# Pooling attention and mixture of depths: first two batches separate, dense work of batch 0 in front of the attention of batch 2, constants on GpSimd

## The chip, the cores and the metric

The kernel runs on one core of one Trainium2 chip. The metric is the device time of the program in microseconds (us). Before the change it is 269.25 us, the median of three runs (268.28, 269.25 and 275.01). The engines of the core are named as in the profile: PE is TensorE, DVE is VectorE, ACT is ScalarE, POOL is GpSimd and SP is SyncE, which here issues the direct DMAs.

## The reference

Two steps follow on each other. First comes an attention in which keys and values are averaged over 8 neighbouring positions; then, for each batch, the 128 rows of the result with the highest gate score go through a two-layer network, and the others stay as they are.

```python
B, H, S, D = 8, 8, 576, 64                       # attention
k_p = k.reshape(B, H, S // 8, 8, D).mean(axis=3)
v_p = v.reshape(B, H, S // 8, 8, D).mean(axis=3)
scores = np.matmul(q, k_p.transpose(0, 1, 3, 2)) / np.sqrt(D)
attn = softmax(scores)                            # + 1e-9 in the denominator
x = np.matmul(attn, v_p)                          # then (B, S, H*D) = (8, 576, 512)
...
scores = np.einsum('bsd,d->bs', x, w_gate)        # mixture of depths
out = x.copy()
for b in range(B):
    top_idx = np.argpartition(-scores[b], 128)[:128]
    xe = x[b, top_idx]
    ye = np.maximum(xe @ w1, 0.0) @ w2            # w1: 512x1024, w2: 1024x512
    g = 1.0 / (1.0 + np.exp(-scores[b, top_idx]))
    out[b, top_idx] = xe + g[:, None] * ye
```

All inputs and the output are float32.

## The kernel before

One function, `direct_path`, holds the whole fast path; a second path runs only if a flag computed at the end asks for it. The schedule is written out by hand: every engine runs its instructions in the order in which the program issues them, and the program issues them in a main loop (L528) over units `u`.

**Units, tiles, chunks.** The 576 positions of a batch are 9 tiles of 64. A unit `u` is three tiles, so a batch has three units, and unit `u` belongs to batch `u // 3`. A chunk `a` is two tiles, 128 rows. Two batches have 18 tiles, so nine chunks; the middle chunk of each pair of batches holds the last tile of the even batch in its lower 64 rows and the first tile of the odd one in its upper 64.

**Attention.** `load_k`, `load_q` and `load_v` issue the input DMAs on SP. `pool_k` (L213) and `pool_v` (L230) add up the eight neighbours, on POOL for all batches but the first; `pool_v` then multiplies the pooled values with the gate weights on POOL, and `gate_v` (L243) sums these products on DVE, so that the gate score comes out of the same matmul as the attention. `k_trans` (L219) and `q_trans` (L263) transpose on DVE. `scores(u)` (L274) runs 32 matmuls into four PSUM banks, and ACT takes the exponential of each bank. `attend(a)` (L287) multiplies the exponentials with the pooled values into an accumulator `pA`, of which there are two; `norm(a)` (L298) takes the reciprocal on DVE and writes the normalised rows `xs` (or `xh` for the middle chunk) and the gate scores `ss`. `store_x(a)` (L331) sends two chunks of rows to the output.

**Choosing rows.** `score(b)` (L350) sums gate scores on DVE, and then splits them into three bf16 parts with five small POOL instructions that write columns 2 to 4 of `auxb` (L362 to L366). `row_bcast(b)` (L368) spreads the scores over rows with five PE transposes into banks 0 and 1. `count(b)` (L374) compares on DVE, with counts in an accumulator output. `one_hot(b)` (L389) sums counts with 15 small matmuls and builds a one-hot matrix on DVE. `gather(b)` (L401) multiplies it with `auxb` on PE (L405), takes the row index (L407, L409) and fetches the chosen rows from the output in DRAM by an indirect DMA on POOL (L413); that DMA waits for the stores of its batch.

**Dense work.** `x_trans(b)` (L425) transposes the fetched rows on PE, `hidden(b, part)` (L432) is the first layer in three parts, `finish(b, part)` (L444) the second in three parts, with an addition on POOL (L454) for each and an indirect DMA back (L456) after the last. `gate(b)` (L419) computes the sigmoid with one small instruction each on ACT, POOL and DVE.

**The order.** `at(u, slot, job)` (L465) puts a job into a slot of a unit. In the main loop a unit runs slot 0, its first chunk (half of it if the unit has only one), slot 1, `scores(u + 1)`, the second chunk (or half), slot 2, the norm, `q_trans(u + 2)`, and then slots 3 to 7. With `w = 3 * (b + 1)`, the unit after the last of batch `b`, the jobs of batch `b` lie from `w` on: `row_bcast` and `count` in slot 3 of `w`, `one_hot` in slot 3 of `w + 1`, `gather` in slot 5 of `w + 1`, `x_trans` in slot 5 of `w + 2`, and the six dense parts in slots 4 and 6 of `w + 3` to `w + 5`. POOL's pooling for batch `b + 2` lies in slots 2 and 5 of `w` and slot 2 of `w + 1`. So three batches are in work at one time. The constants of the choosing are computed on DVE by `constants()` (L177) in slot 3 of unit 0. Each dense or choosing step names its PSUM bank by hand (`nb`).

Of the kernel before, what the change touches and what calls it, by code (L numbers as in the profile page):

```python
# [48 lines left out]
def direct_path(ctx, tc, q, k, v, moe_w_gate, moe_w1, moe_w2, moe_capacity, out, flag):  # L49
# [20 lines left out]

    nc = tc.nc
# [23 lines left out]
    NCH = B * NT // 2  # L95
# [21 lines left out]

    nc.vector.memset(vraws[0], 0.0)
    nc.gpsimd.memset(vraws[1], 0.0)
# [10 lines left out]
    load_q(0)  # L130
    load_v(0, 0)
# [23 lines left out]
    for t in kts + vps + vraws[2:]:  # L155
        nc.gpsimd.memset(t, 0.0)
# [20 lines left out]
    def constants():  # L177
        nc.vector.tensor_scalar(ident, diff, 0.0, None, op0=OP.is_equal)
        nc.vector.tensor_scalar(before[:, NC - 2, :], diff, 0.0, None, op0=OP.is_lt)
        nc.vector.memset(ones, 1.0)  # L180
        nc.vector.memset(one32, 1.0)

        ge, q16, q4, hi = (const.tile([C, n], FT, name=x) for x, n in (
            ("ge", C // G - 1), ("q16", 1), ("q4", 1), ("hi", 1)))
        nc.vector.tensor_scalar(ge, steps, 0.0, None, op0=OP.is_ge, op1=OP.add, accum_out=q16)
        nc.vector.tensor_scalar(q4, q16, 4.0, None, op0=OP.mult)
        nc.vector.scalar_tensor_tensor(hi, q16, -float(G), part, op0=OP.mult, op1=OP.add)
        nc.vector.tensor_scalar(hi, hi, float(TG), None, op0=OP.mult)
        for i, a in enumerate(auxb):
            nc.vector.tensor_scalar(a[:, 0 : NC - 1, 0], numbers, 0.0, hi, op0=OP.mult, op1=OP.add)  # L190
            nc.vector.tensor_copy(a[:, NC - 1, 0:1], hi)
            nc.vector.tensor_scalar(a[:, i : i + NC - 1, 1], numbers, q4, None, op0=OP.add)  # L192
            h = (NC - 1) * (1 - i)
            nc.vector.tensor_scalar(a[:, h, 1:2], q16, float(32 - 4 * i), None, op0=OP.add)
# [10 lines left out]
    def bank(i, shape):  # L205

        return psum.tile(shape, FT, name=f"bank{i}", bufs=1)
# [22 lines left out]
    def pool_v(b, g, eng):  # L230
        x = VR[b, g]
        VP[b] = vps[b % 2]
        h = slice(HG * g, HG * g + HG)
        if eng is nc.vector:
            eng.tensor_reduce(out=VP[b][:, h, 0:D], in_=x.rearrange("p h t d -> p h d t"), axis=AX.X, op=OP.add)
        else:
            eng.tensor_tensor(out=x[:, :, 0:4, :], in0=x[:, :, 0:4, :], in1=x[:, :, 4:8, :], op=OP.add)  # L237
            eng.tensor_tensor(out=x[:, :, 0:2, :], in0=x[:, :, 0:2, :], in1=x[:, :, 2:4, :], op=OP.add)  # L238
            eng.tensor_tensor(out=VP[b][:, h, 0:D], in0=x[:, :, 0, :], in1=x[:, :, 1, :], op=OP.add)

        nc.gpsimd.tensor_tensor(out=x[:, :, 2, :], in0=VP[b][:, h, 0:D], in1=wg[:, h, :], op=OP.mult)
# [5 lines left out]


# [25 lines left out]
    def scores(u):  # L274
        b = u // NTH
        p = [bank(i, [128, 2, TS * TL]) for i in range(4)]
# [10 lines left out]
    def attend(a, heads=range(H)):  # L287
        if heads[0] == 0:
            PA[a] = psum.tile([C, 2, 512], FT, name="pA")
        for h in heads:  # L290
            g, n = divmod(h, HG)
            for t in range(2):
                u, i = divmod(2 * a + t, TS)
                nc.tensor.matmul(PA[a][TL * t : TL * t + TL, g, E * n : E * n + E],  # L294
                                 ET[u][h // 2][:, h % 2, TL * i : TL * i + TL], VP[u // NTH][:, h, :],
                                 start=True, stop=True)

    def norm(a):  # L298
        o = PA.pop(a)[:, :, 0 : HG * E].rearrange("p g (n d) -> p g n d", d=E)
        rz = rzall[:, a, :].rearrange("p (g n) -> p g n", g=2)  # L300
        if a % NT == 0:
            SS[a // NT] = work.tile([C, NT, H], FT, name="ss")
        nc.vector.reciprocal(rz, o[:, :, :, D])  # L303
        k = a % NT
        if k == NC - 1:
            XS[a] = work.tile([C, 1, DM], FT, name="xh")
        elif k - (k >= NC) in (0, 2, 4, 6):
            XS[a] = work.tile([C, 2, DM], FT, name="xs")
        else:
            XS[a] = XS[a - 1]  # L310
        nc.vector.tensor_tensor(out=XS[a][:, 0 if XS.get(a - 1) is not XS[a] else 1, :].rearrange("p (g n d) -> p g n d", g=2, d=D), in0=o[:, :, :, 0:D],  # L311
                                in1=rzall[:, a, :].rearrange("p (g n one) -> p g n one", g=2, one=1).to_broadcast(
                                    [C, 2, HG, D]), op=OP.mult)
        nc.vector.tensor_tensor(out=SS[a // NT][:, a % NT, :].rearrange("p (g n) -> p g n", g=2),
                                in0=o[:, :, :, D + 1], in1=rz, op=OP.mult)
# [15 lines left out]
    def store_x(a):  # L331
# [5 lines left out]
        b = 2 * (a // NT)  # L337
        k = a % NT
        if k == NC - 1:
            x = XS[a][:, 0, :]  # L340
            for n in range(2):
                put(b + n, out[b + n].rearrange("(g t) d -> t g d", g=G)[32:TG], x[TL * n : TL * n + TL])
        elif XS.get(a - 1) is XS[a]:
            b += k >= NC
            i = (k - 1) % NC if k < NC else k - NC - 1
            x = XS[a].rearrange("p i d -> p (i d)")
            y = out[b].rearrange("(g t) d -> g t d", g=G)[:, 0:32].rearrange("g (t i) d -> t g i d", i=4)
            put(b, y[:, :, i : i + 2, :].rearrange("t g i d -> t g (i d)"), x)
# [568 lines left out]
```

## Time and profile before

| what | value |
|---|---|
| median of three runs | 269.25 us |
| the profiled execution: its time, its span | 272.41 us, 270.6 us |
| PE busy, share of the span | 223.3 us, 83% |
| PE weight loads busy | 207.3 us, 77% |
| POOL busy | 155.1 us, 57% |
| DVE busy | 137.6 us, 51% |
| ACT busy | 66.5 us, 25% |
| DMA | 46.94 MB, 173 GB/s over the span |

The page's map of the span in 40 slices (6.8 us each) shows where each engine works; a digit is the busy share in tenths, and PEclk is the granted TensorE clock in tenths:

```profile
PE   0396176680699999999999999999999999999970
PEclk9999669656589999999999999999999999999995
DMA  7999997876702636686736276831222203301101
```

From left to right: PE is thinly used in the first ten slices and full in nearly all others. The DMA engines are full in the first seven slices. The granted clock falls to five or six tenths around slices 5 to 6 and 8 to 11.

### The profile page before, as it was taken

What the parts mean: (1) busy time and instruction counts of PE and PEld (TensorE: products, weight loads), DVE (VectorE), ACT (ScalarE), POOL (GpSimd) and SP (SyncE); (2) the same over time, 40 slices, a digit from 0 to 9 for tenths busy, and PEclk for the clock granted to TensorE, in tenths of its full rate; (3) what the DMA queues carried; (4) which work ended last, traced back from release to release, by engine and by line L of the source; (5) the groups of instructions that cost most, each with busy time, mean ns of one, the idle gap of its engine ahead of it and who ended that gap; (6) DMA issues with size and microseconds to landing.
All of it is one profiled execution on the core that took longest, in us unless ns stands there. A gap on an engine that the chain in (4) does not pass through costs nothing.

```text
span 270.6 us, 7289 instructions
## 1 busy us (share of the span) xinstructions
PE 223.3 (83%) x3050; PEld 207.3 (77%) x3050; DVE 137.6 (51%) x387; ACT 66.5 (25%) x162; POOL 155.1 (57%) x193
## 2 busy tenths in 40 slices
PE   0396176680699999999999999999999999999970
PEld 0376165580599799889997998899889999999970
DVE  7859936664064537654755476538554733411000
ACT  2042022211033133323332333223322331212210
POOL 9889706967970229973995299639953103313021
PEclk9999669656589999999999999999999999999995
DMA  7999997876702636686736276831222203301101
GB/s 278 344 354 398 398 354 284 323 274 204 277 13 50 236 88 206 226 263 208 271 65 249 79 217 224 267 95 44 48 71 79 80 18 116 104 2 39 41 0 51
DMA packets 13048, 46.94 MB, mean 173 GB/s; under 512 B 1104, under 2 KB 1104, under 8 KB 10960
## 3 DMA queue, kind: packets, MB, share of 16 engines
q1 hardware_dynamic: 11728, 42.21, 46.1%
q0 software_dynamic: 1280, 4.20, 4.7%
q8 instruction: 26, 0.43, 0.7%
q14 instruction: 14, 0.11, 0.1%
HBM read 34.87 MB, written 11.53 MB: 171 GB/s over the span
## 4 chain that ended last, share of the span: by engine, by line
PE 69%; DVE 13%; DMA 8%; issue 4%; POOL 3%; ACT 0%; POOLq 0%; DVEq 0%
PE bank L452 21%; PE bank L440 18%; PE bank L281 14%; PE pA L294 13%; DMA out_dram<-xs 5%; DVE qt L271 3%; DMA xr<-out_dram,idx 3%; DVE oh L397 2%; PE bank L371 2%; PE bank L428 2%; DVE xs L311 1%; DVE auxb L192 1%; DVE vp L203 1%; PE bank L405 1%; DVE ge L386 1%
## 5 line engine op out<-in xcount | busy, mean ns | idle before, releaser
L281 PE MATMUL bank<-qt,kt 32*128 32x192 f32 x768 | 46.6, 380 | 18.3 <-DVE qt L271 11.7
L440 PE MATMUL bank<-xg,w 128*128 128x128 f32 x512 | 60.5, 277 | 0.0
L452 PE MATMUL bank<-w,ht 128*128 128x176 f32 (+1 forms) x384 | 60.2, 311 | 0.0
L285 ACT ACTIVATE et<-bank 128x384 f32<-128x384 f32 x96 | 39.4, 495 | 81.9 <-PE bank L281 81.9
L440 PEld LDWEIGHTS bank<-xg,w 128*128 128x128 f32 x512 | 58.4, 192 | 0.5 <-ACT et L285 0.5
L452 PEld LDWEIGHTS bank<-w,ht 128*128 128x128 f32 x384 | 55.8, 190 | 0.6
L294 PEld LDWEIGHTS pA<-vp,et 128*64 128x64 f32 x1152 | 42.4, 152 | 15.7 <-issue 14.9
L281 PEld LDWEIGHTS bank<-qt,kt 32*128 32x128 f32 x768 | 38.6, 216 | 20.6 <-POOL sc L168 11.2
L294 PE MATMUL pA<-vp,et 128*64 128x66 f32 x1152 | 49.0, 241 | 6.1 <-DVE rzall L303 4.7
L303 DVE RECIPROCAL rzall<-pA 128x8 f32<-128x8 f32 x36 | 7.5, 207 | 80.3 <-PE pA L294 80.3
L237 POOL TENSOR_TENSOR vraw<-vraw 128x1024 f32<-128x1024 f32 x15 | 35.3, 2354 | 0.9 <-DVE qt L271 0.9
L454 POOL TENSOR_TENSOR y<-y,xr 128x176 f32<-128x176 f32 (+1 forms) x24 | 13.1, 548 | 39.4 <-ACT y L453 39.0
L271 DVE STREAM_TRANSPOSE qt<-qraw 128x512 f32<-128x512 f32 (+1 forms) x48 | 24.5, 551 | 0.0
L442 ACT ACTIVATE ht<-bank 128x384 f32<-128x384 f32 (+1 forms) x24 | 10.9, 456 | 51.9 <-PE bank L440 51.9
L311 DVE TENSOR_TENSOR xs<-pA,rzall 128x512 f32<-128x512 f32 x32 | 22.1, 691 | 1.4 <-DVE rzall L303 0.2
L453 ACT ACTIVATE y<-bank,g 128x176 f32<-128x176 f32 (+1 forms) x24 | 9.7, 403 | 51.2 <-PE bank L452 51.2
L409 POOL TENSOR_SCALAR idx<-tok 128x1 int32<-128x1 f32 x8 | 1.9, 244 | 31.6 <-DVE g L411 31.4
L238 POOL TENSOR_TENSOR vraw<-vraw 128x512 f32<-128x512 f32 x15 | 19.1, 1272 | 1.2
L386 DVE SCALAR_TENSOR_TENSOR ge<-bank,sc,before 128x128 bf16<-128x128 f32 (+3 forms) x40 | 18.2, 498 | 1.6 <-PE bank L371 1.6
L216 POOL TENSOR_TENSOR kraw<-kraw 128x1152 f32<-128x1152 f32 x7 | 18.4, 2634 | 0.1
L362 POOL CAST auxb<-sc 128x5 bf16<-128x5 f32 x8 | 1.6, 202 | 21.1 <-DVE sc L358 10.7
L428 PE MATMUL bank<-ident,xr 128*128 128x128 f32 x32 | 5.3, 292 | 9.2 <-DMA xr<-out_dram,idx 9.2
(85 smaller groups left out, 186.0 us busy)
## 6 DMA issues: line engine op xcount, KB each, us to landing
kraw<-in_k_dram SPq DMA_DIRECT2D x8, 1152.0 KB
qraw<-in_q_dram SPq DMA_DIRECT2D x8, 1152.0 KB
vraw<-in_v_dram SPq DMA_DIRECT2D x16, 512.0 KB
out_dram<-xs SPq DMA_DIRECT2D x16, 512.0 KB
w<-in_moe_w_dram SPq DMA_DIRECT2D x2, 2048.0 KB
vraw<-in_v_dram SPq DMA_DIRECT2D x16, 64.0 KB
out_dram<-xh SPq DMA_DIRECT2D x8, 128.0 KB
wg<-in_moe_w_gate_dram SPq DMA_DIRECT2D x1, 256.0 KB
```

The source lines that it names most:

```text
L216: eng.tensor_tensor(out=x[:, :, 0:2, :], in0=x[:, :, 0:2, :], in1=x[:, :, 2:4, :], op=OP.add)
L237: eng.tensor_tensor(out=x[:, :, 0:4, :], in0=x[:, :, 0:4, :], in1=x[:, :, 4:8, :], op=OP.add)
L238: eng.tensor_tensor(out=x[:, :, 0:2, :], in0=x[:, :, 0:2, :], in1=x[:, :, 2:4, :], op=OP.add)
L271: nc.vector.transpose(out=QT[u][:, :, n : n + m, :].rearrange("p j t c -> p t j c"), in_=x)
L281: nc.tensor.matmul(p[i][:, s, :], KT[b][r, j, s, :], QT[u][r, j, :, G * s : G * s + G], start=(j == 0), stop=(j == 1))
L285: nc.scalar.activation(ET[u][i], p[i], AF.Exp, scale=exp_scale)
L294: nc.tensor.matmul(PA[a][TL * t : TL * t + TL, g, E * n : E * n + E], ET[u][h // 2][:, h % 2, TL * i : TL * i + TL], VP[u // NTH][:, h, :] ...
L311: nc.vector.tensor_tensor(out=XS[a][:, 0 if XS.get(a - 1) is not XS[a] else 1, :].rearrange("p (g n d) -> p g n d", g=2, d=D), in0=o[:, :, ...
L386: nc.vector.scalar_tensor_tensor(x, y, s, m, op0=OP.is_ge, op1=OP.mult, accum_out=CN[b][:, c : c + 1])
L440: nc.tensor.matmul(p[:, n, :], w1[:, d, 128 * f : 128 * f + 128], XG[b][:, d, :], start=(d == 0), stop=(d == DB - 1))
L452: nc.tensor.matmul(p, HT[b][:, f, :], w2[:, f, c], start=(f == 0), stop=(f == FB - 1))
L454: nc.gpsimd.tensor_tensor(out=Y[b][:, c], in0=Y[b][:, c], in1=XR[b][:, c], op=OP.add)
```

## The change

Five things are changed.

- **The first two batches are split.** The middle chunk of the first pair becomes two chunks of 64 rows, so that batch 0 is complete without a tile of batch 1 (37 chunks instead of 36). Batch 0 is scored one unit earlier.
- **The jobs of batches 0, 1 and 2 get slots of their own.** All dense work of batch 0 is put into unit 5, before the attention of batch 2. The dense work of batches 1 and 2 is spread over units 6 to 10 and 11 to 14. Later batches keep their slots. The loop runs slots up to 12. `w2` is loaded in unit 2 instead of unit 1.
- **The score parts become a job of their own, `parts(b)`,** in the slot of `one_hot(b)`, for all batches. `gate(b)` comes after `x_trans(b)` in the same slot.
- **Constants move from DVE to POOL,** ahead of the first loop; three zero fills move from POOL to ACT; the pooling of v for batch 0 is done on DVE in additions. `scores(1)` moves into the loop.
- **`row_bcast` uses a `pA` accumulator** instead of banks 0 and 1; the other steps take the four banks in turn. The counts go into a zeroed tile `cn` and are summed by one reduction.

```diff
-    NCH = B * NT // 2
+    NCH = B * NT // 2 + 1
...
+    for t in vraws[1:]:
+        nc.scalar.memzero(t.rearrange("p h t d -> p (h t d)"))
...
-    for t in kts + vps + vraws[2:]:
+    for t in kts + vps:
         nc.gpsimd.memset(t, 0.0)
...
-    def constants():
-        nc.vector.tensor_scalar(ident, diff, 0.0, None, op0=OP.is_equal)
...
+    nc.gpsimd.memset(rzall[:, NC - 1 : NC + 1, :], 1.0)
+    cn = [const.tile([C, NC, 2], FT, name=f"cn{i}") for i in range(2)]
+    for t in cn:
+        nc.gpsimd.memset(t, 0.0)
+    nc.gpsimd.tensor_scalar(ident, diff, 0.0, None, op0=OP.is_equal)
+    nc.gpsimd.tensor_scalar(before[:, NC - 2, :], diff, 0.0, None, op0=OP.is_lt)
...
+    nc.gpsimd.tensor_scalar(steps, steps, 0.0, None, op0=OP.is_ge)
+    nc.gpsimd.tensor_copy(q16, steps[:, 0:1])
+    for i in range(1, C // G - 1):
+        nc.gpsimd.tensor_tensor(out=q16, in0=q16, in1=steps[:, i : i + 1], op=OP.add)
...
+    turn = [0]
+
+    def bank(shape, i=None):
+
+        if i is None:
+            i = turn[0]
+        turn[0] = (i + 1) % 4
         return psum.tile(shape, FT, name=f"bank{i}", bufs=1)
...
+    CH = []
+    for i in range(B * NT // 2):
+        if i == NT // 2:
+            CH += [(2 * i, None), (None, 2 * i + 1)]
+        else:
+            CH.append((2 * i, 2 * i + 1))
...
+    def parts(b):
 
         a = auxb[b % 2]
+        s = scs[b % 2]
         r1 = work.tile([C, NC], FT, name="r1")
         nc.gpsimd.tensor_copy(a[:, :, 2], s)
...
     def row_bcast(b):
-        SR[b] = [bank(0, [C, NC - 1, C]), bank(1, [C, 1, C])]
+        p = psum.tile([C, 2, 512], FT, name="pA")
+        SR[b] = [p[:, 0, :].rearrange("p (c i) -> p c i", i=C), p[:, 1, 0:C].rearrange("p (c i) -> p c i", i=C)]
...
-        nc.vector.tensor_tensor(out=CN[b][:, NC - 1 : NC], in0=CN[b][:, NC - 1 : NC], in1=CN[b][:, NC : NC + 1], op=OP.add)
+        nc.vector.tensor_reduce(out=CN[b], in_=k, axis=AX.X, op=OP.add)
...
-            at(u + 1, 2, store_x, a)
+            at(*((u + 1, 2) if u != 5 else (u, 5)), store_x, a)
...
-        at(*((w - 1, 3) if b % 2 else (w, 1)), score, b)
-        at(w, 1 if last else 3, row_bcast, b)
-        at(w, 1 if last else 3, count, b)
-        at(*((w, 7) if last else (w + 1, 3)), one_hot, b, 0)
-        at(w + 1, 5, gather, b, 3)
-        at(w + 2, 5, gate, b)
-        at(w + 2, 5, x_trans, b, 2)
-        at(w + 3, 4, hidden, b, 0, 2)
...
+        at(*((w - 1, 3) if b % 2 or b == 0 else (w, 1)), score, b)
+        steps_of = {
+            0: dict(row_bcast=(3, 1), one_hot=(4, 1), gather=(4, 3), x_trans=(5, 3),
+                    dense=((5, 4), (5, 6), (5, 7), (5, 9), (5, 11), (5, 12))),
+            1: dict(row_bcast=(5, 5), one_hot=(5, 8), gather=(5, 10), x_trans=(6, 5),
+                    dense=((6, 6), (7, 4), (8, 4), (9, 4), (9, 6), (10, 4))),
+            2: dict(row_bcast=(9, 3), one_hot=(10, 3), gather=(10, 5), x_trans=(11, 3),
+                    dense=((11, 4), (11, 6), (12, 4), (13, 4), (13, 6), (14, 4))),
+            B - 1: dict(row_bcast=(w, 1), one_hot=(w, 7), gather=(w + 1, 5), x_trans=(w + 2, 5)),
+        }.get(b, dict(row_bcast=(w, 3), one_hot=(w + 1, 3), gather=(w + 1, 5), x_trans=(w + 2, 5)))
+        dense = steps_of.get("dense", [(w + 3 + i // 2, 4 + 2 * (i % 2)) for i in range(6)])
+        at(*steps_of["row_bcast"], row_bcast, b)
+        at(*steps_of["row_bcast"], count, b)
+        at(*steps_of["one_hot"], parts, b)
+        for f in (one_hot, gather, x_trans):
+            at(*steps_of[f.__name__], f, b)
+        at(*steps_of["x_trans"], gate, b)
+        for i, x in enumerate(dense):
+            at(*x, (hidden, finish)[i // 3], b, i % 3)
...
-    at(1, 0, lambda: nc.sync.dma_start(out=w2, in_=moe_w2.rearrange("(a p) n -> p a n", p=128)))
+    at(2, 3, lambda: nc.sync.dma_start(out=w2, in_=moe_w2.rearrange("(a p) n -> p a n", p=128)))
     eights()
-    pool_v(0, 0, nc.gpsimd)
...
+    pool_v(0, 0, nc.vector)
+    pool_v(0, 1, nc.vector)
     q_trans(1)
-    scores(1)
-    pool_v(0, 1, nc.vector)
...
-    at(0, 3, constants)
...
-        if 0 < u < NU - 1:
+        if u < NU - 1:
             scores(u + 1)
...
-        for slot in range(3, 8):
+        for slot in range(3, 13):
             run(u, slot)
```

`attend`, `norm`, `store_x` and `score` are rewritten for the list `CH` of chunks; what they compute per tile stays.

## The prediction

> **What bounds the kernel now.** I read the page first, then busy time by stretch, the list of waits, the chain that ended last, and the timelines of 0 to 90 and 90 to 135 us. Columns of the first view: stretch and its length, busy time per engine, granted TensorE clock, DMA share, GB/s.
>
> ```profile
> core 0: us, PE busy (x) PEld busy (x) DVE busy (x) ACT busy (x) POOL busy (x), PEclk, DMA share, GB/s
> 11.00:21.00 10.00, 9.26 (x106) 8.35 (x108) 5.62 (x7) 3.28 (x8) 9.12 (x7) 1.00 1.01 345
> 21.00:30.00 9.00, 4.02 (x92) 3.54 (x88) 8.86 (x24) 1.64 (x4) 8.69 (x7) 0.94 1.02 400
> 30.00:44.00 14.00, 9.75 (x163) 8.65 (x164) 7.72 (x23) 2.88 (x8) 3.14 (x9) 0.67 0.96 349
> 44.00:58.00 14.00, 8.05 (x129) 6.99 (x130) 11.39 (x32) 2.06 (x6) 13.45 (x10) 0.69 0.84 307
> 58.00:70.30 12.30, 3.09 (x61) 2.75 (x57) 3.50 (x12) 1.72 (x5) 8.03 (x12) 0.64 0.71 256
> 97.00:124.00 27.00, 26.44 (x399) 24.66 (x398) 15.82 (x46) 8.16 (x20) 19.26 (x22) 1.00 0.63 201
> ```
>
> Two regimes. From 70.3 us to the tail TensorE (PE) is full: 26.4 of 27.0 us for one batch. Before that it is busy for 34.2 of 70.3 us, much of it at a low clock. Time can only come from the first 70 us; any new PE wait afterwards costs its full length. Three waits, each met once, shape the early part (total, times, longest):
>
> ```profile
> POOL auxb L362 <- DVE sc L355: 10.4, 1, 10.4
> ...
> PE bank L428 <- DMA xr<-out_dram,idx: 9.2, 1, 9.2
> ...
> POOL xr L413 <- issue: 3.5, 1, 3.5
> ```
>
> GpSimd (POOL) stood 10.4 us at 32 us for batch 0's scores, with batch 2's pooling queued behind. So the index of the first gather came only at 58.21; its transfer waited 3.46 us for no visible reason and took 8.24; PE stood until 70.29. Now a later batch, around the matmuls that read the one-hot (L405):
>
> ```profile
> 102.50 0.20 POOL L362 CAST auxb<-sc 128x5 bf16<-128x5 f32 x1
> ...
> 103.73 2.63 POOL L216 TENSOR_TENSOR kraw<-kraw 128x1152 f32<-128x1152 f32 x1
> ...
> 115.55 0.28 PE L405 MATMUL bank<-auxb,oh 128*128 128x5 bf16 x5 [0.56 <-DVE oh L397]
> ...
> 117.66 0.68 POOL L241 TENSOR_TENSOR vraw<-vp,wg 128x256 f32<-128x256 f32 x1
> 118.43 0.25 POOL L409 TENSOR_SCALAR idx<-tok 128x1 int32<-128x1 f32 x1
> ```
>
> The reader is to see the order on POOL: the score parts (L362 to L366) run **before** 14.5 us of pooling, so L405, which reads them as auxb, does not wait for POOL. The pooling itself ends at 118.3, later than L405.
>
> **What the Trainium skill says.** "TensorE: Matmul & The Clock Gate", section on the array's architectural detail: GpSimd serves its queue strictly in order, and so do ScalarE and VectorE; the 10.4 us above agree. The same page, Part 1: after an idle window of about 3.4 us PE runs at half clock, for about as long once busy again; the trace grants 0.50 from 65 to 75 us, after the stand from 62, and 32 score matmuls take 2.9 us against 1.51 warm. "GPSIMD Engine Reference", section 3: an addition of two tensors is about 1.96 times as slow on GpSimd as on VectorE; here 2637 against 1359 ns (L216), 1.94. Its section 2.1 puts a first call after loading code at about 6 us; the first gather's 3.46 us may be of that kind, which no run shows.
>
> **Part by part, the early phase.** Prices are rows of the page unless said.
>
> Memsets: three of 1.8 us leave POOL for ScalarE. ScalarE has no such row; its copies of 512 and 384 columns (586, 495 ns) extrapolate to 1.7 us, so from 0.7 to about 7.5 us with the 1.28 table load. Its first exponential is at 14.14: 0, and at double price still under 14.
>
> Constants: 6.5 us leave VectorE (22.7 to 29.2 us in the chain). 26 small instructions go to POOL, spaced 0.27 as L362 to L366 are: 7 us. POOL starts 5.4 us earlier for want of the memsets, so it ends near 12.5; its next work, the gate product, needs VectorE's pooling at 13.5. Cost 0; at twice the price first attention slips 6 us.
>
> Pooling v of batch 0: VectorE does it in additions. L216 and L217 give 1.04 ns a column plus 0.16 us: 1.22 + 0.69 + 0.42 = 2.3 us a half, from the landings at 11.1 and 13.1, so to 15.8. Then q_trans(1) 0.95 and gate sums 0.82: 17.6 us, against 17.98. scores(1) now stands between the halves of the first attention, so norm(0) is at 22.4 rather than 20.8.
>
> From there I follow each queue in program order with these prices: a norm 1.05 (L303, L311, L314), q_trans 0.95, k_trans 2.1, counting 3.7 on VectorE; scores 1.5 warm or 2.9 cold, full-chunk attention 1.1 on PE; the four exponentials 1.64. norm(0) and q_trans(2) end at 24.4, exponentials of unit 1 at 23.2, attend(1) at 24.3: norm(1) starts at 24.4 (was 29.1). norm(1), norm(2), q_trans(3) and k_trans(1) on VectorE follow on each other, the second after attend(2) at 27.1: k_trans(1) ends 31.3 (33.9). Then norm(3), gate sum, norm(4), q_trans(4), the scores' sums and the other gate sum reach 36.4; the split chunk adds norm(5), 1.05 us; count(0) runs from 37.5 (45.8). Counting now holds one of the two pA accumulators: attend(7) waits for it until 41.2. One-hot ends at 44.3, and scores(5) waits that long for bank 0; index at 49.1 (58.2). POOL doesn't hold it: parts go behind pool_k(2), and with w2 off SP's queue ahead of them k2 and v2 land about 6 us earlier (2 MB at 345 GB/s), so the pooling of batch 2 ends near 47. w2 lands by 46 and is needed near 73; the stores of batch 0 that it delays land near 47, before the gather.
>
> Repeating the gather's 3.46 + 8.24 us gives x_trans(0) at **61.2**, 9.1 us earlier. Ends: a landing of 3.4 us, this row's minimum, and no 3.46 give 53, where attention still holds PE until 55; a gather no earlier than before gives 70. After it come 0.7 for the XG copy, now uncovered, a cold start (1.5), dense(0) 14.6 and batch 1's counting matmuls: stage u=6 starts near 80 and u=9 at 97.1. The old u=9 started at 100.0, with 7.3 us less of dense done. **Lead 10 us.**
>
> **The late phase.** `parts` moves from `score` to the one-hot's slot, past pool_k, pool_v(.,0) and pool_v(.,1) of batch b+2 on POOL. L405 now waits for these. Using the stage prices 2.75 or 3.7 (attention), hidden 2.68, 2.68, 1.9, finish 2.5, 2.6, 2.2, pooling 4.05 + 5.1 + 5.1, parts 1.3:
> - Batch 2: in POOL's order pool_v(4,0) is behind the addition of finish(1,0), so it starts 8 us into u=9 and parts end at 20.1; PE is at the gather at 15.0. Wait 5.1. The index is then behind an addition and a scatter (1.7), and x_trans(2), moved up to slot 3, waits 2.4 more: 7.5.
> - Batch 3: PE has finish(2,0) in front; parts are 0.8 early: 0.
> - Batch 4: 2.5. Batch 5: 2.6. In the timeline above: POOL from 102.5, pooling to 117.0, parts to 118.3, less 115.55, is 2.75. Batches 6 and 7 have no pooling ahead: 0.
>
> Sum 12.6, less the waits for the one-hot that it swallows (0.6 in four batches): **10.2 lost**. The cold restart after 5 us of standing would add up to 1.7; part of it lies under the wait for x_trans(2): take 1. Below nothing isn't possible: nothing speeds L405. If POOL keeps 3 us more slack it is 4; if each wait is 1.5 longer, 17.
>
> At no cost: the count's last sum (L387, 946 ns) becomes a single-input reduction of some 0.15 us; gate after x_trans holds VectorE about 0.8 us longer. VectorE is busy 15.8 of 27 us, and PE's work covers both. The pA lent to counting is free 3.4 us before the second attention of the next stage needs it (108.6 against 112.0). The banks taken in turn are read before scores want them.
>
> Sum: 270.6 - 10 + 10.2 + 1 = 271.8 span. The profiled execution took 272.41, 3.2 above the median of 269.25; carried over, 270.5. Following the queues ignores small waits: **271**.
>
> **Rivals.** (A, 0.48) As above, gain given back: 271, own range 265 to 275. (B, 0.18) POOL arrives in time, or the first gather lands in 3 to 4 us, so the lead survives: 269.25 - 9.5 = 260. For it: batch 3's slot shows that a PE job in front suffices; against: POOL's pooling ended 2.8 us after L405 already, without the parts behind it. (C, 0.34) The parts' wait outweighs the lead. Place: L405 of batches 2, 4, 5. Price 12.6, or 17 with cold restarts. It decides once the waits exceed the lead by 5.4. With the gather at 66 (lead 5.5), the end is 269.25 + 17 - 5.5 - 2.4 = 278. For it: transfers still fill the DMA engines (0.96 to 1.02) when that gather runs. That dense(0) gets ahead of little, since PE still stands for the gather from 54.5 to 61, is inside A.
>
> **Numbers.** 2% is about what a measurement of this kernel tells from no change: 263.9 and 274.6. A is mostly inside, B faster, C slower: 0.18, 0.48, 0.34. Range 261 to 281: A with most of B and C.
>
> **What would show it.** Right: POOL's 10.4 us gone; first gather's index at 47 to 52 us; x_trans(0) at 59 to 63; L405 waiting for POOL auxb L366 in three late batches, 2 to 5 us each, and PE under 25 of 27 us there. Wrong: no late wait of L405 on POOL (then B), or x_trans(0) after 66 (then C).

## The result, and the profile after

The changed kernel takes 279.38 us, the median of four runs (278.65 to 282.01); the kernel before, run beside it, took 272.13 us (268.28 to 276.58). The ratio is **1.043, 95% interval 1.033 to 1.052: slower**. (A ratio compares undisturbed runs of both kernels only, so here and below it is the quotient neither of the medians nor of the spans: the one profiled execution of the kernel before, 272.41 us, is 3 to 4 us longer than its undisturbed runs of 268.28 and 269.25, while the changed kernel's, 279.86, is 0.5 above its median.) The profiled execution took 279.86 us with a span of 278.1 us, against 272.41 and 270.6 before.

The map of the span, in 40 slices of 7.0 us, for the changed kernel:

```profile
PE   0358566639998999478999995999789999999980
...
PEclk9999879777999999959999998899979999999997
DMA  7999999878120739745745587230312204301101
```

The reader is to see two things. PE is full from slice 10, or 63 us (before: from slice 12, or 74 us). But now there are holes after it, at slices 17, 25 and 29 (from 111, 167 and 195 us), and the granted clock dips at the same places or just behind them. Before, nothing of the kind followed the first 80 us.

Busy time by stretch (stretch and length, PE, PE weight loads, DVE, ACT, POOL, then granted clock, DMA share, GB/s), changed kernel:

```profile
core 0: us, PE busy (x) PEld busy (x) DVE busy (x) ACT busy (x) POOL busy (x), PEclk, DMA share, GB/s
21.00:30.00 9.00, 6.41 (x152) 5.33 (x148) 5.52 (x14) 3.28 (x8) 8.69 (x7) 1.00 1.01 410
...
58.00:70.30 12.30, 8.89 (x57) 8.52 (x58) 4.36 (x17) 1.18 (x3) 1.21 (x6) 0.72 0.77 290
97.00:124.00 27.00, 21.65 (x325) 20.19 (x325) 14.54 (x45) 6.51 (x16) 18.91 (x22) 0.88 0.61 201
```

From 21 to 30 us DVE is no longer full (5.52 us busy, before 8.86), and PE does 6.41 us of work instead of 4.02. From 58 to 70.3 us PE does 8.89 us instead of 3.09. From 97 to 124 us it loses: 21.65 us at a clock of 0.88, where it had 26.44 at 1.00. The list of waits (total, times, longest) of the changed kernel names the cause:

```profile
PE bank L435 <- POOL auxb L394: 11.7, 3, 5.4
...
PE bank L458 <- DMA xr<-out_dram,idx: 3.7, 1, 3.7
POOL xr L443 <- POOL idx L439: 3.6, 7, 0.8
```

L435 is the gather matmul (L405 before), L394 the last score part. Its three waits are new. The 10.4 us for which POOL stood for the scores are gone, the wait for the first gathered rows fell from 9.2 to 3.7 us, and the 3.5 us ahead of the first gather's transfer fell to 0.83. (In the ten traces of the experiments this last wait is 0.7 to 1.8 us, so the 3.5 belongs to the one profiled execution before.) The chain that ended last, by engine, says the same in one line:

```profile
PE 56%; POOL 22%; DVE 8%; issue 5%; DMA 5%; ACT 1%; POOLq 0%; DVEq 0%; ACTq 0%
```

POOL has 22% of it; before it had 3%, and PE 69%.

**The early phase, as forecast.** The timeline around the first gather:

```profile
50.84 0.24 POOL L439 TENSOR_SCALAR idx<-tok 128x1 int32<-128x1 f32 x1 [2.71 <-DVE g L441]
51.91 1.23 POOL L443 DMA_INDIRECT xr<-out_dram,idx  x1 [0.83 <-POOL idx L439]
60.74 1.09 PE L458 MATMUL bank<-ident,xr 128*128 128x128 f32 x4 [3.68 <-DMA xr<-out_dram,idx]
```

x_trans(0) starts at 60.74 us, 9.55 earlier than in the profiled execution before (70.29).

**The late phase.** POOL around the gather matmul of batch 2:

```profile
107.05 0.56 POOL L484 TENSOR_TENSOR y<-y,xr 128x176 f32<-128x176 f32 x1 [5.90 <-ACT y L483]
107.56 2.35 POOL L245 TENSOR_TENSOR vraw<-vraw 128x1024 f32<-128x1024 f32 x1
...
117.88 0.68 POOL L249 TENSOR_TENSOR vraw<-vp,wg 128x256 f32<-128x256 f32 x1
118.51 0.20 POOL L390 CAST auxb<-sc 128x5 bf16<-128x5 f32 x1
...
119.58 0.20 POOL L394 CAST auxb<-r 128x5 bf16<-128x5 f32 x1
```

And PE, in batches 2, 4 and 5 (the last bracket is the idle time before, and for whom); below it, the place of batch 4 in the kernel before:

```profile
112.04 2.44 PE L482 MATMUL bank<-w,ht 128*128 128x160 f32 x16
119.84 0.28 PE L435 MATMUL bank<-auxb,oh 128*128 128x5 bf16 x5 [5.35 <-POOL auxb L394]
120.04 2.03 PE L315 MATMUL pA<-vp,et 128*64 128x66 f32 x32
122.00 2.70 PE L301 MATMUL bank<-qt,kt 32*128 32x192 f32 x32
...
171.35 0.27 PE L435 MATMUL bank<-auxb,oh 128*128 128x5 bf16 x5 [3.05 <-POOL auxb L394]
171.48 4.31 PE L482 MATMUL bank<-w,ht 128*128 128x176 f32 x16
...
202.97 0.27 PE L435 MATMUL bank<-auxb,oh 128*128 128x5 bf16 x5 [3.34 <-POOL auxb L394]
203.10 4.18 PE L482 MATMUL bank<-w,ht 128*128 128x176 f32 x16
```

```profile
169.29 0.28 PE L405 MATMUL bank<-auxb,oh 128*128 128x5 bf16 x5 [0.56 <-DVE oh L397]
169.43 2.63 PE L452 MATMUL bank<-w,ht 128*128 128x176 f32 x16
```

In batch 2 POOL first stands 5.90 us for the input of an addition of batch 1, then works through 11 us of pooling and one more addition, and only then writes the parts; PE stands for the last 5.35 us of this. And the price does not end with the wait. What comes right behind it is slow: 2.03 and 2.70 us for pieces that take 1.16 and 1.58 elsewhere, 4.31 and 4.18 for 16 matmuls of the second layer that take 2.63 in the same places before. The granted clock is 0.57 from 172 to 176 us. Such slow work at a lower clock behind a stand is called a slow or cold restart below.

A subtraction sorts all runs below. Before, 200.3 us lie between the start of x_trans(0) and the end (270.6 - 70.29). In the changed kernel it is 217.4 us (278.1 - 60.74). So the change wins **9.55 us** up to there and loses **17.1 us** after it, which makes the 7.5 us of the two spans. In both kernels PE has the same 2513 matmuls left at that point; the changed kernel is busy with them for 4.6 us more (193.7 against 189.2) and idle for 12.5 us more.

The ratio says more than 7.5: some 11.5 us. The difference is the profiled execution before, which was 3 to 4 us too long. Kernels 7 and 10 below have its code behind x_trans(0) and take 200.2 and 201.9 us there, so the excess most likely lies ahead of it. By this estimate the change wins about 6 us, not 9.55, against the shorter runs, and the loss of 17.1 stands.

### The profile page after: what moved, and what is told of

Read it like the earlier page. It is cut to its first block, busy times and chain, and to the rows that moved or that the text cites. A ratio compares the mean times of both kernels' runs of the same rounds, so it can differ in the third digit from the quotient of the medians.

```text
span 278.1 us, 7308 instructions
## 1 busy us (share of the span) xinstructions
PE 225.4 (81%) x3050; PEld 209.9 (75%) x3050; DVE 126.1 (45%) x378; ACT 72.2 (26%) x165; POOL 155.1 (56%) x213
## 4 chain that ended last, share of the span: by engine, by line
PE 56%; POOL 22%; DVE 8%; issue 5%; DMA 5%; ACT 1%; POOLq 0%; DVEq 0%; ACTq 0%
PE bank L482 19%; PE bank L470 16%; PE bank L301 9%; PE pA L315 9%; POOL vraw L245 6%; POOL vraw L246 4%; DMA xr<-out_dram,idx 3%; POOL kraw L227 3%; POOL vraw L249 2%; POOL vp L247 2%; DMA kraw<-in_k_dram 2%; DVE qt L291 2%; POOL ks L228 2%; PE pA L400 1%; PE bank L458 1%
## 5 line engine op out<-in xcount | busy, mean ns | idle before, releaser
L470 PE MATMUL bank<-xg,w 128*128 128x128 f32 x512 | 62.6, 282 | 2.3 <-ACT xg L460 2.3
L482 PE MATMUL bank<-w,ht 128*128 128x176 f32 (+1 forms) x384 | 63.1, 322 | 0.0
L470 PEld LDWEIGHTS bank<-xg,w 128*128 128x128 f32 x512 | 60.2, 197 | 3.4 <-ACT xg L460 3.2
L301 PE MATMUL bank<-qt,kt 32*128 32x192 f32 x768 | 45.2, 379 | 20.5 <-DVE qt L291 11.2
L482 PEld LDWEIGHTS bank<-w,ht 128*128 128x128 f32 x384 | 59.0, 198 | 0.4
L328 DVE RECIPROCAL rzall<-pA 128x8 f32<-128x8 f32 (+1 forms) x37 | 7.6, 205 | 84.8 <-PE pA L315 84.8
L245 POOL TENSOR_TENSOR vraw<-vraw 128x1024 f32<-128x1024 f32 x14 | 33.0, 2357 | 0.0
L416 DVE SCALAR_TENSOR_TENSOR ge<-pA,sc,before 128x128 bf16<-128x128 f32 (+3 forms) x40 | 18.3, 501 | 5.5 <-PE pA L400 5.5
L435 PE MATMUL bank<-auxb,oh 128*128 128x5 bf16 x40 | 2.2, 167 | 11.8 <-POOL auxb L394 11.7
L249 POOL TENSOR_TENSOR vraw<-vp,wg 128x256 f32<-128x256 f32 x16 | 10.9, 683 | 1.2
```

Source lines behind the costliest of these rows:

```text
L301: nc.tensor.matmul(p[i][:, s, :], KT[b][r, j, s, :], QT[u][r, j, :, G * s : G * s + G], start=(j == 0), stop=(j == 1))
L416: nc.vector.scalar_tensor_tensor(x, y, s, m, op0=OP.is_ge, op1=OP.mult, accum_out=k[:, c, 0:1])
L470: nc.tensor.matmul(p[:, n, :], w1[:, d, 128 * f : 128 * f + 128], XG[b][:, d, :], start=(d == 0), stop=(d == DB - 1))
L482: nc.tensor.matmul(p, HT[b][:, f, :], w2[:, f, c], start=(f == 0), stop=(f == FB - 1))
```

## The experiments

My theory after the result: the early part brings a lead, the moved `parts` lose it in the late phase. The rivals: the split chunk, the new slots or the dense work put ahead cost the time; or it is the clock alone. Ten experiments (7 and 10 are one kernel), each with runs of the kernel before on its own chip; the three columns of times are of the one profiled execution of each:

| kernel | x_trans(0), us | from there to the end | span | ratio to before, 95% |
|---|---|---|---|---|
| before | 70.29 | 200.3 | 270.6 | 1 |
| changed | 60.74 | 217.4 | 278.1 | 1.043 (1.033 to 1.052) |
| 1: parts early, rest changed | 62.95 | 216.9 | 279.8 | 1.049 (1.029 to 1.069) |
| 2: before, parts late | 64.14 | 217.1 | 281.2 | 1.057 (1.045 to 1.069) |
| 3: gather of batches 4, 5 behind finish | 60.44 | 210.6 | 271.0 | 1.015 (0.999 to 1.030) |
| 4: pooling and parts of batch 2 earlier | 61.88 | 211.6 | 273.5 | 1.011 (1.000 to 1.023) |
| 5: as 4, with work ahead of x_trans(2) | 61.63 | 205.5 | 267.1 | 0.989 (0.978 to 1.000) |
| 6: added matmuls keep PE busy | 63.05 | 217.1 | 280.1 | 1.033 (1.021 to 1.045) |
| 7: before, early part alone | 62.51 | 200.2 | 262.7 | 0.985 (0.970 to 1.001) |
| 10: the same again | 62.41 | 201.9 | 264.3 | 0.987 (0.981 to 0.993) |
| 8: as 7, rows and counts as changed | 60.88 | 200.9 | 261.8 | 0.975 (0.970 to 0.980) |
| 9: batch 0 ahead, later slots as before | 58.97 | 205.7 | 264.7 | 0.997 (0.994 to 1.000) |

Seven kernels have the changed kernel's code up to x_trans(0) (changed, 1, 3, 4, 5, 6, 9), and it lies between 59.0 and 63.1 us in them: a difference of two microseconds in that column is not to be read by itself.

**1. The parts behind the scores again, the rest as changed**

```diff
+        if b >= 2:
+            at(*((w - 1, 3) if b % 2 else (w, 1)), parts, b)
...
-        at(*steps_of["one_hot"], parts, b)
+        if b < 2:
+            at(*steps_of["one_hot"], parts, b)
```

> The changed kernel with one thing undone for batches 2 to 7: the five score parts are issued on GpSimd directly behind the sums of score, ahead of the pooling of batch b+2, as in the kernel before. Theory (the parts' place in GpSimd's queue costs the late phase): the waits of L435 for auxb of 3.05 us (batch 4) and 3.3 us (batch 5) go, with the cold restarts behind them (finish(b,0) took 4.2 and 4.0 us instead of 2.5), so about 9.5 us. Batch 2 gains only about 1 us, since its index is still behind pool_v(4,1) and its x_trans is two slots earlier. Span 278.1 - 10 = 268, ratio to before 0.97 to 1.00. Rival (the slots of batches 0 to 2, or the accumulator lent to counting, are the cost): the waits move elsewhere, span 275 or more, ratio 1.02 or more.

282.33 us, ratio 1.049: missed, and the waits moved elsewhere, as the rival had it. All waits of L435 for POOL are gone. But a new one stands in batch 2 (timeline of this kernel):

```profile
116.41 0.28 PE L435 MATMUL bank<-auxb,oh 128*128 128x5 bf16 x5 [0.16 <-DVE oh L427]
...
123.23 1.07 POOL L443 DMA_INDIRECT xr<-out_dram,idx  x1 [0.29 <-POOL idx L439]
123.47 0.34 SPq L111 DMA_DIRECT2D kraw<-in_k_dram  x1
123.92 2.36 SPq L125 DMA_DIRECT2D vraw<-in_v_dram  x1
...
133.98 1.09 PE L458 MATMUL bank<-ident,xr 128*128 128x128 f32 x4 [12.68 <-DMA xr<-out_dram,idx]
```

L435 now runs on time, but the index is still behind POOL's pooling, and x_trans(2) was moved to one unit behind it. The gather leaves at 123.23 us, 0.24 us ahead of the loads of batch 5, and its rows take 10.6 us; the shortest landing in this trace is 3.3. In the changed kernel these loads came only at 127.97, behind a store of attention rows that PE's stand had delayed to 126.80; the gather, issued at 122.23, landed in 3.8 us. One wait was taken away and the one behind it came up, larger. The moved slots of batch 2 are a second fault, hidden behind the first. (That the loads slow the rows is read from these times; no run moves the loads alone.)

**2. The kernel before, with `parts` in the slot of `one_hot` and nothing else**

```diff
+    def parts(b):
+        s = scs[b % 2]
         a = auxb[b % 2]
...
+        at(*((w, 7) if last else (w + 1, 3)), parts, b)
         at(*((w, 7) if last else (w + 1, 3)), one_hot, b, 0)
```

> The kernel before with that one thing done: the score parts are put into the slot of the one-hot, behind the pooling of batch b+2, nothing else. Theory: L405 waits 2.2 to 2.8 us for the parts in each of batches 2 to 5, with about 1.5 us of cold restart behind each and 0.6 us of one-hot wait saved: 4 x 3.4 = 13.6 us slower; the 10.4 us wait of GpSimd at 32 us goes, but gains at most 1 us, since VectorE's chain holds the first gather. Ratio 1.03 to 1.06. Rival (the slots of batches 0 to 2 are the cost): ratio 0.99 to 1.01.

283.39 us, ratio 1.057: as expected. Its PE timeline at batch 4:

```profile
174.51 0.27 PE L408 MATMUL bank<-auxb,oh 128*128 128x5 bf16 x5 [3.37 <-POOL auxb L369]
174.63 4.31 PE L455 MATMUL bank<-w,ht 128*128 128x176 f32 x16
```

Here the sum can be closed. The gather matmul (now L408) stood 3.38, 2.58, 3.37 and 2.56 us in batches 2 to 5, 11.9 in all (the second and fourth are put down to DVE's k_trans, which ended in the same moment as POOL's last part: both at 143.71 in batch 3); less the 0.56 to 0.63 it stood there before, 9.5. The second-layer piece behind it took 5.04, 4.31, 4.31 and 4.04 instead of 2.63: 7.2 more. Together 16.7 us, and the kernel is 16.8 us longer behind x_trans(0) (217.1 against 200.3). Two fifths of the price is the slow restart.

The same edit also took POOL's early stand away, and x_trans(0) came 6.2 us earlier than in the profiled execution before. But the index came only 0.7 us earlier (57.55), as expected. The rest is the transfer: 0.70 us ahead of it instead of 3.46, and 5.50 to land instead of 8.24. So POOL's stand of 10.4 us was not what held the first gather.

**3. The gather of batches 4 and 5 behind the second-layer piece, the rest as changed**

```diff
+        if b in (4, 5):
+            steps_of["gather"] = (w + 1, 7)
```

> The changed kernel with the parts where it has them, but the gather matmul of batches 4 and 5 moved two slots back, behind finish(b-1,0), so that TensorE has 2.5 us of work while the parts are made. Theory (a wait with nothing in front costs its length and a cold restart): the two waits shrink from 3.05 and 3.3 to under 1 us and finish(b-1,0) runs in 2.5 us, so 2 x (2.5 + 1.6) = 8 us: span 270, ratio 0.98 to 1.01. Rival (GpSimd itself is the bound in the late phase, so any order on TensorE ends the same): span 276 or more.

272.36 us, span 271.0, 7.1 us less than the changed kernel: as expected in the span and the mechanism; the ratio of 1.015 lies just above the range. PE at batch 4:

```profile
169.07 2.55 PE L482 MATMUL bank<-w,ht 128*128 128x176 f32 x16
172.31 0.27 PE L435 MATMUL bank<-auxb,oh 128*128 128x5 bf16 x5 [0.69 <-POOL auxb L394]
```

With 2.5 us of other PE work ahead of it, L435 waits 0.69 us for its parts here and 1.02 in batch 5, and the second-layer piece runs in 2.55. The parts are as late as in the changed kernel; only PE's order differs.

**4. Pooling and parts of batch 2 earlier on POOL**

```diff
+        if b >= 3:
+            at(*((w - 1, 3) if b % 2 else (w, 1)), parts, b)
...
-            at(u, 5, pool_v, b + 1, 0, nc.gpsimd)
+            at(u, 3 if u == 9 else 5, pool_v, b + 1, 0, nc.gpsimd)
...
+    at(9, 3, parts, 2)
```

> As the first kernel for batches 3 to 7; and for batch 2, pool_v(4,0) is put in front of the addition of finish(1,0) in GpSimd's queue, with the parts of batch 2 behind it, so that GpSimd doesn't stand 5.9 us at 101 us for that addition. Theory: the wait of L435 in batch 2 (5.35 us) and the cold attention behind it (about 2 us) go too; x_trans(2) may wait 1 to 2 us for its rows. Span 261 to 264, ratio 0.955 to 0.985: faster than before. Rival (the slots of batches 0 to 2 are the cost): 270 or more.

272.24 us, ratio 1.011 (the profiled execution, 275.27, was the longest of its four): missed, about half of the gain that was expected, and the number is the rival's. No wait of L435 is over 0.7 us, but x_trans(2), in its moved slot, waits 4.93 us for rows that took 6.6 to land, and hidden(2) behind it is slow again: its 48 matmuls took about 8.5 us, and 5.5 elsewhere.

**5. The same, with work ahead of x_trans(2)**

```diff
-                    dense=((6, 6), (7, 4), (8, 4), (9, 4), (9, 6), (10, 4))),
+                    dense=((6, 6), (7, 4), (8, 4), (9, 4), (10, 4), (11, 3))),
...
-            at(u + 1, 3, k_trans, b + 1)
+            at(u + 1, 6 if u == 9 else 3, k_trans, b + 1)
```

> The fourth kernel, with x_trans(2) given cover: finish(1,1) and finish(1,2) move to slot 4 of unit 10 and slot 3 of unit 11, the latter in front of x_trans(2), and k_trans(4) moves behind the gather of batch 2, so that its index isn't late. Theory (what was left in the fourth kernel is the 4.9 us wait of x_trans(2) for its rows and the half clock behind it, hidden(2) 8.5 us instead of 5.4): the wait falls under 2 us and hidden(2) runs in 5.4 to 6: 5 to 7 us less than the fourth kernel. Ratio 0.97 to 0.99. Rival (the transfer is only pushed into the loads of batch 5 and ends as late): ratio 1.00 to 1.02.

268.11 us, ratio 0.989: as expected.

```profile
123.69 0.63 PE L458 MATMUL bank<-ident,xr 128*128 128x128 f32 x4 [1.93 <-DMA xr<-out_dram,idx]
124.99 5.62 PE L470 MATMUL bank<-xg,w 128*128 128x128 f32 x48 [0.68 <-ACT xg L460]
```

The wait of x_trans(2) is down to 1.93 us, though its rows took 7.3 to land, and hidden(2) takes 5.62.

**6. Work for PE during the wait.** In batches 4 and 5, 16 matmul calls on the weights, whose result nothing reads, run ahead of the gather matmul of the changed kernel.

```diff
     def gather(b):
+        if b in (4, 5):
+            i = turn[0]
+            p = bank([cap, 176], i)
+            for f in range(FB):
+                for n in range(2):
+                    nc.tensor.matmul(p, w2[:, f, 128 * n : 128 * n + 128], w2[:, f, 0:176],
+                                     start=(f == 0 and n == 0), stop=(f == FB - 1 and n == 1))
+            turn[0] = i
```

> The changed kernel with 16 added matmuls of the shape 128x176 that nothing reads (2.5 us) in front of the gather matmul of batches 4 and 5. TensorE still waits for the same parts, but is busy for most of the wait. Theory (each wait of 3 us has a second price, a cold restart): parts end when they did, so L435 isn't earlier, but finish(b-1,0) behind it runs in 2.5 us instead of 4.2 and 4.0: 3.2 us less in all, ratio 1.02 to 1.035. Rival (no clock effect, the long finish has another cause): finish(b-1,0) stays at 4 us, ratio as the changed kernel's, 1.04.

279.81 us. PE at batch 4:

```profile
169.86 4.94 PE L438 MATMUL bank<-w 128*128 128x176 f32 x32
174.94 0.27 PE L442 MATMUL bank<-auxb,oh 128*128 128x5 bf16 x5
175.07 2.63 PE L489 MATMUL bank<-w,ht 128*128 128x176 f32 x16
```

The added work came out twice as large as meant (the profile counts 32 matmuls), and outlasts the parts, which were written at 173.06, by 1.8 us; so the total tells nothing. The last line does: behind PE that was kept busy the second-layer piece takes 2.63 us, behind PE that stood 3.05 us it took 4.31. (In batch 5 it is 2.63 against 4.18.) From 172 to 176 us the granted clock is 1.00 here and 0.57 in the changed kernel. The restart's price is shown: 1.7 us at this place.

**7. The early part alone.** The kernel before, with the zero fills on ACT, the constants on POOL, the pooling of v for batch 0 by additions on DVE, `scores(1)` in the loop, `w2` in unit 2, all as the change has them, and the late `parts` for batch 0 only. No split chunk, no dense work ahead, slots and banks as before.

```diff
+        if b > 0:
+            parts(b)
...
+        if b == 0:
+            at(w + 1, 3, parts, b)
         at(*((w, 7) if last else (w + 1, 3)), one_hot, b, 0)
```

> The kernel before with the early part of the change alone: constants on GpSimd in the preamble, zero fills on ScalarE, pooling of v of batch 0 on VectorE, scores(1) in the loop, w2 loaded in unit 2, the score parts of batch 0 (only) in the one-hot's slot. Chunks, slots, banks and all other parts stay. Theory (the lead of the changed kernel comes from VectorE and GpSimd being free early, which brings the first gather forward): the first gather's index at 50 to 54 us instead of 58.2, x_trans(0) at 61 to 65 instead of 70.3, span 262 to 266, ratio 0.97 to 0.985. Rival (without the split of the middle chunk and the earlier slots nothing comes forward): x_trans(0) after 68, ratio 0.99 to 1.00.

265.48 us, ratio 0.985: as expected. From x_trans(0) to the end it is the kernel before to 0.1 us (200.2 and 200.3), so the whole gain is the earlier x_trans(0). By the ratio the gain is some 4 us; the 7.8 us between the two profiled executions hold the excess of the one before.

**8. Rows in a pA accumulator and counts in a zeroed tile, on top of 7**

```diff
-        SR[b] = [bank(0, [C, NC - 1, C]), bank(1, [C, 1, C])]
+        p = psum.tile([C, 2, 512], FT, name="pA")
+        SR[b] = [p[:, 0, :].rearrange("p (c i) -> p c i", i=C), p[:, 1, 0:C].rearrange("p (c i) -> p c i", i=C)]
...
-        nc.vector.tensor_tensor(out=CN[b][:, NC - 1 : NC], in0=CN[b][:, NC - 1 : NC], in1=CN[b][:, NC : NC + 1], op=OP.add)
+        nc.vector.tensor_reduce(out=CN[b], in_=k, axis=AX.X, op=OP.add)
```

> The early part alone (median ratio 0.985 in the run before this one, span 262.7) plus two things that the forecast set at no cost: rows for counting in a pA accumulator, and the counts in a zeroed tile summed by one reduction. My theory (no cost, since PE work covers both): span 262 to 264, ratio within 0.01 of the early part alone, which runs beside it. Rival (the pA lent to counting holds the attention back in every batch): 0.5 us or more a batch, span 267 or more, with new waits of the attention matmuls for DVE.

262.60 us, ratio 0.975 (0.970 to 0.980), with 0.987 (0.981 to 0.993) for the early part alone beside it: better than no cost. The intervals do not meet. The scores of unit 5 show where gain comes from; first in the kernel without the two edits (experiment 10), then in this one:

```profile
44.96 3.12 PE L280 MATMUL bank<-qt,kt 32*128 32x192 f32 x32 [3.64 <-DVE ge L387]
```

```profile
43.73 1.58 PE L283 MATMUL bank<-qt,kt 32*128 32x192 f32 x32 [0.16 <-DVE qt L273]
```

In the old order the scores of unit 5 wait 3.64 us for DVE to finish counting in banks 0 and 1, and then run cold. With the rows in pA they run at once. The two edits were not tried apart: the last sum of the counts also fell, from 886 ns in the mean to 166, once a batch on DVE. This is the fastest kernel of this case.

**9. Batch 0 split and its dense work ahead, later slots as before**

```diff
-            1: dict(row_bcast=(5, 5), one_hot=(5, 8), gather=(5, 10), x_trans=(6, 5),
-                    dense=((6, 6), (7, 4), (8, 4), (9, 4), (9, 6), (10, 4))),
-            2: dict(row_bcast=(9, 3), one_hot=(10, 3), gather=(10, 5), x_trans=(11, 3),
-                    dense=((11, 4), (11, 6), (12, 4), (13, 4), (13, 6), (14, 4))),
+            1: dict(row_bcast=(5, 5), one_hot=(5, 8), gather=(5, 10), x_trans=(8, 5)),
```

and `parts` as in 1.

> The changed kernel with the score parts right behind the scores from batch 2 on, and batches 1 and 2 with their dense work (and x_trans) in the slots of all later batches; only batch 0 keeps its own completion and its dense work ahead of the attention of batch 2. Theory that the split and the dense work ahead are worth about as much as the early part alone, and that all of the loss sits in the moved parts and the moved slots of batches 1 and 2: unit 9 begins at 91 to 93 us, span 262 to 266, ratio 0.97 to 0.985. Rival (with dense work of batch 0 out of units 6 to 8, PE there outruns POOL's pooling of batch 3, 14.5 us from about 80): PE waits for keys of batch 3 ahead of unit 9, unit 9 begins at 96 or later, span 267 to 270, ratio 0.99 to 1.0.

268.88 us, ratio 0.997: the span of its one profiled execution, 264.7, is where it was expected, but that was the fastest of 19 runs (266.55 to 272.83), and the ratio missed. So this order is worth nothing that can be seen against before, and is 2.3% slower than kernel 8 on the same chip (0.997 / 0.975). Unit 9 begins at 92.2, as expected; but ahead of it and within it PE waits:

```profile
89.45 1.58 PE L301 MATMUL bank<-qt,kt 32*128 32x192 f32 x32 [3.62 <-DVE kt L239]
...
95.25 0.65 PE L315 MATMUL pA<-vp,et 128*64 128x66 f32 x14 [2.24 <-DVE g L453]
```

The first is for the keys of batch 3: with no dense work between, PE runs ahead of DVE, where the transposition of the keys is queued behind a norm and q_trans. The second is put down to `gate` (L453), but the gate sums of batch 3 run on DVE just ahead of it, from 94.68 us, and had waited for POOL's last product, which ended at 94.65. POOL could begin that batch's pooling only at 80.04, after the last step of the dense work put ahead, and needs 14.6 us for it: the bound that the rival named.

**10. The early part again, with more rounds**

> The early part alone once more, with more rounds, on the chip of the two others: its interval touched 1.0 before. Expected ratio 0.97 to 0.985, span 262 to 264. If the first result was luck of one chip: 0.99 to 1.0.

266.22 us, span 264.3, ratio 0.987 (0.981 to 0.993): just above both expected ranges (ratio and span), but the whole interval lies below 1. A gain of 0.7 to 1.9% is shown on a second chip.

Together: the parts' place alone costs the kernel before 16.8 us behind x_trans(0) (2), by waits that PE can cover (3) and restarts that need PE to stand (6). The rivals are right in part. The moved slots of batch 2 are a second fault (1, 4, 5), and the split chunk with the dense work ahead brings nothing over kernel 8 (9).

## Why the prediction was wrong

The forecast was "gain given back" at 271 us, and 279.38 were measured; what happened is its rival C, the parts' wait outweighing the lead, at its upper price. The place and the cause of the waits were right; terms of the sum were mis-sized, the slow restart most of all.

- **Zero fills on ScalarE, cost 0:** right. They ran from 2.02 to 7.5 us, as worked out.
- **Constants on GpSimd, ending near 12.5:** they ended at 16.14, and the next gate product began at 16.22. Some of the small instructions took 0.7 to 1.3 us instead of 0.2 to 0.3 (last section). It cost nothing visible: norm(0) was forecast at 22.4 and came at 22.41.
- **The early queues:** norm(1) at 24.4 (24.28), k_trans(1) done by 31.3 (31.1), index at 49.1 (50.84), x_trans(0) at 61.2 (60.74). The chain was 1.7 us late by the index; the 3.46 us that I repeated ahead of the transfer were only 0.83, its landing 8.69 instead of 8.24. The two roughly cancelled. That POOL's stand of 10.4 us held the first index was a wrong reading: without it the index came 0.7 us earlier (experiment 2); with DVE freed as well it came at 53.33 (experiment 7). Experiments 7 and 8 show which parts made the lead: by the ratios the early part some 4 us, the rows in pA with the new counts some 3 more. With the split chunk as well x_trans(0) came at 59.0 to 63.1, around the 60.88 of experiment 8, so the split itself bought nothing that can be seen.
- **"Lead 10 us" at u=9:** u=6 began at 79.8, as forecast ("near 80"), but u=9 at 99.66, not 97.1: units 6 to 8 took 19.9 us, not the 17.1 from 80 to 97.1. x_trans(1) waited for the exponentials (0.50), its first reader for the copy (0.98), the scores of unit 9 for the keys (0.62). The lead was 0.34 + 7.3 = 7.6 us.
- **L405 waits for batches 2, 4, 5 and not 3:** right in place, in all four. Batch 2: 5.1 forecast, 5.35 measured. Batches 4 and 5: 2.5 and 2.6, measured 3.05 and 3.34.
- **The failing step: "The cold restart after 5 us of standing ... take 1".** I counted one restart, behind the longest wait, and let x_trans(2) swallow part of it. The runs show three: about 2.0 us behind batch 2 (0.87 + 1.12), 1.68 behind batch 4, 1.55 behind batch 5. That is 5.2 us instead of 1. Experiment 6 shows it by itself, and experiment 2 closes its sum only with it. From u=9 on, 15.1 us were lost where 10.2 + 1 were forecast: the restarts cost 4.2 more and the waits of L435 1.5 more, while the 2.4 for x_trans(2) did not come. With the lead 2.4 short, that is 6.3 us, and 271.8 + 6.3 is the measured span of 278.1.
- **The excess of 3.2 us carried over:** the span was forecast 6.3 us too short, but the time 8.4. The profiled execution before was 3.2 us above the median, and I took this off the changed kernel too, whose profiled execution was only 0.5 above. If the excess lies ahead of x_trans(0), as estimated above, it was in the lead already and was taken off twice.
- **x_trans(2) waits 2.4 more:** in the changed kernel it hardly waits; PE's own stand delays the loads that come beside its rows in experiment 1. That was luck: with the stand gone, it waits 12.7 us there.
- **"At no cost":** the counts' reduction takes 166 ns (946 before), right. The rows in pA, tried together with it, were not neutral but a gain, which I missed: they free the banks that the next scores wait for. The banks in turn and the gate behind x_trans cost nothing visible; neither was tried alone.
- **Rival C's price** was 17 us with cold restarts: 17.1 measured from x_trans(0) on. I gave it an example with a lead of only 5.5 because of a late gather. The gather was not late, and the lead of 9.55 by the profiled executions was not enough either; against the shorter runs it was about 6 by the estimate above, and the end close to the 278 of that example.

On the restart, the Trainium skill ("TensorE: Matmul & The Clock Gate", Part 1) says that PE falls to half clock after an idle window of about 3.4 us. I read this as a threshold that waits of 2.5 us stay under. The trace disagrees with that reading: stands of 2.56 to 3.38 us (experiment 2) already made the next 16 matmuls 1.4 to 2.4 us longer. Nor is it certain above that length: behind the stand of 3.62 us in experiment 9 the granted clock stayed at 1.00 (89 to 93 us) and the 32 score matmuls took 1.58 us. So the length of a stand alone does not tell whether a restart follows. Here the measurement decides.

What stays open: why kernel 9 scatters over 6 us and the kernel before over 10, while kernel 8, run beside them, scatters over 2.7; where the last 5 us of kernel 5 behind x_trans(0) go (205.5 against 200 to 202); and whether kernel 8 gains from a split chunk with slots made for it. This was not tried, nor were the split and the dense work ahead tried apart.

## What to carry to other kernels

When a small step is moved behind long work on another engine's queue, price its wait where PE stands, and allow for a slow restart behind each such stand, even of 2.6 us: in experiment 2 it was two fifths of the loss, though one stand of 3.6 us in experiment 9 had none. Compare the profiled execution with the other runs of its kernel before taking a lead from it. Put other PE work between the late input and its reader (experiment 3 got 7.1 us back in this way without making the input earlier), and look at what the wait you remove was holding back (experiment 1). And take a bundle of edits apart: two groups of its parts were worth 2.5% (experiment 8), and the rest cost more than that.

## What the runs showed of the hardware

**Small instructions on POOL or DVE can last as long as a long one beside them on the other engine.** POOL's constants and DVE's work of the changed kernel, from its timelines:

```profile
6.07 1.32 POOL L188 TENSOR_SCALAR steps<-steps 128x7 f32<-128x7 f32 x1
...
11.02 1.23 POOL L198 CAST auxb<-hi 128x1 bf16<-128x1 f32 x1
...
13.48 1.21 POOL L197 TENSOR_SCALAR auxb<-numbers,hi 128x4 bf16<-128x4 f32 x1
```

```profile
5.92 1.36 DVE L227 TENSOR_TENSOR kraw<-kraw 128x1152 f32<-128x1152 f32 x1 [1.31 <-DMA kraw<-in_k_dram]
...
11.03 1.18 DVE L245 TENSOR_TENSOR vraw<-vraw 128x1024 f32<-128x1024 f32 x1
...
13.34 1.22 DVE L245 TENSOR_TENSOR vraw<-vraw 128x1024 f32<-128x1024 f32 x1
```

Each of these POOL instructions, of one to seven columns, ends within 0.15 us of a DVE addition of two tensors (11.02 + 1.23 and 11.03 + 1.18, for instance); beside other DVE work the same kinds take 0.2 to 0.3 us. The Trainium skill ("GPSIMD Engine Reference", Specifications) says that GpSimd shares its SBUF interfaces with VectorE, with contention when a DVE instruction has two SBUF inputs; the trace agrees, and shows that a short instruction may wait for the whole of the long one.

It goes the other way too. In the kernel before, while DVE computed the constants:

```profile
26.83 2.32 DVE L192 TENSOR_SCALAR auxb<-numbers,q 128x4 bf16<-128x4 f32 x1
```

```profile
26.79 2.34 POOL L237 TENSOR_TENSOR vraw<-vraw 128x1024 f32<-128x1024 f32 x1
```

Five of the small DVE instructions there took 5.8 of the 6.5 us, and each of the five ended within 0.1 us of a POOL instruction with two tensor inputs; the other small ones between them took 0.14 to 0.22 us. So what moving the constants gave back to DVE was mostly such waiting.

**The landing of an indirect gather of 128 rows varied threefold.** It took 3.4 us at the least in the kernel before, 8.69 for the first one of the changed kernel, with the DMA engines 81% busy meanwhile, and 10.6 when the loads of a batch followed 0.24 us after it (experiment 1). With those loads 5.3 us after it (experiment 5) it still took 7.3, so their start alone does not set it, and no run varied it by itself.
